# Attention with a relative bias, then a mixture of adapters: a new order of the opening's transfers and key tiles, and 1 KB pieces of k for seven more pairs

## The chip, the cores and the metric

The kernel runs on one core of one Trainium2 chip. The metric is the device time of one execution in microseconds (us), as the median of several runs; less is better.

## The reference

```python
# attention: q, k, v are (B=8, H=8, S=576, D=64) fp32, bias_table is (32, 8)
scores = q @ k.T / sqrt(64)                       # per batch and head, 576 x 576
bucket = f(abs(i - j))                            # 32 buckets, the last one from distance 128 on
scores = scores + bias_table[bucket]              # per head
attn = exp(scores - max); attn = attn / sum
attn_out = attn @ v
# mixture of adapters: x is attn_out as (N=4608, Dm=512); 8 experts of rank 16, two per row
logits = x @ w_gate                               # (512, 8)
w = softmax over the two largest logits of a row
delta = sum over the two chosen e of w_e * (x @ A[e]) @ B[e]
out = x + delta                                   # (4608, 512) fp32
```

The bias depends only on the distance between two positions, and from 128 on it is one constant per head, which cancels in the softmax.

## The kernel before

**Units of work.** Two heads of one batch are a pair; there are 32 pairs, `u` = 0 to 31, four per batch. Of the 576 positions of a head, 512 are the main part, worked on as four tiles of 128 keys in the order `KO = (0, 3, 1, 2)`; the other 64 are the tail. The tail's 64 keys against all main queries, and its 64 queries against all main keys, are the "edges" of a pair; tail against tail is a "corner".

**What is done for one pair.** `load` issues the transfers of q, k and v on SP's DMA queue into staging buffers (four per tensor). `cast` makes bf16 of them, on POOL for most pairs. `turn` has TensorE (PE) transpose k and q, with the tails and what the adapters need, into a PSUM score tile (L396), and VectorE (DVE) copies the result to SBUF as `tx` (L401). `keys(u, c)` makes the scores of one key tile (L459), adds the bias by further matmuls from the table `W` (L464), and has ScalarE (ACT) take the exponential (L467, into `pk`). `edges(u)` does the same for the edges (L516, L519, exponential L521 into `pt`), whose bias is multiplied in afterwards by `edge_l` on POOL (L526) and `edge_t` on DVE. `step(u, j)` makes the values of one half of the queries (L545, L553, L562, L564 into `pv`), divides by the sums on DVE (L584, L585, giving the rows `xn`) and takes in pieces of the adapters' work (L592, L648).

**Shared memory.** There are three PSUM score tiles, used in a ring by `keys`, `edges` and `turn`. Two further PSUM banks (`mm`) are shared by the values, the adapters' products and the edge factors. v has three bf16 buffers.

**Two ways to load k.** q, and the k of the pairs below `WHOLE = 10`, are loaded with one transfer of 256 KB in which partition p holds positions 4p to 4p+3, so that each piece is 1 KB. v, and k from pair 10 on, are loaded with two transfers of 128 KB in pieces of 256 B, in which partition p holds positions p, 128+p, 256+p and 384+p. A k that was loaded whole has to be put in order: in `turn`, its item is then named `keys_done`, the copy to SBUF is split in two, and the first part (L399, 512 elements per partition) reorders the four key blocks while the second (L401) copies the rest.

**The bias table.** It is built on chip, written to a DRAM buffer `g_d`, and read back for the second to fourth pair of each batch by `table(h)` (L212, two transfers into `Wt`, issued on SP). From `Wt`, ACT makes exponentials for the edge factors (`near_first` for the first pair; `near_rows`, L206, for the other three), and POOL makes a reordered copy `W` by `split_table` (L216), which the bias matmuls of all pairs but the first read. `factors_l` makes the edge factors `EL` and `EC` with small matmuls into both `mm` banks (L238, L244) and DVE copies (L248); `factors_t` makes `ET` in the same manner (L257).

**Order.** The order on every engine is written out by hand: each engine runs its instructions in the order of the program text, and SP issues its transfers in that order. The opening is a list of calls. Its transfers stand in one block:

```python
load(2, "qk")
load(0, "v"); load_tail(0, "v")
for h in range(2): table(h)
load(3, "qk"); load(1, "v"); load(4, "qk"); ...
```

and behind the turn of the third pair the calls follow in the order that the diff shows. From pair 2 to pair 29 a loop runs: casts of pair u+2, issue of the loads of q and k of pair u+4 and v of pair u+3, key tiles 0, 3 and 1 of pair u, `step(u-1, 0)`, key tile 2, `turn` of pair u+2, the edges of pair u+1, `step(u-1, 1)`. A pair's turn is thus done two passes before its keys are. The edges of pair u+1 stand inside `turn`, behind its copies, save where the flag `behind` is true: there the turn brings the tails of a batch whose first pair is u+1, and the edges follow `step(u-1, 1)`. That is so at u = 3 alone, since the tails of the later batches are turned a pass or more ahead of their first use.

Of the kernel before, what the change touches and what calls it, by code (L numbers as in the profile page):

```python
# [37 lines left out]
def kernel(  # L38
# [11 lines left out]
    nc = tc.nc  # L50
# [38 lines left out]
    NU = len(units)  # L89


    WHOLE = 10
    NV = 3
    PT = 64 + 2 * SM
    vts = [cp.tile([128, 4, 2, W1], BF16, name=f"v{i}", tag=f"v{i}") for i in range(NV)]
# [6 lines left out]
    def load(u, names="qkv", eng=nc.sync):  # L102
        b, hp = units[u]
        for nm in names:
            src = {"q": q, "k": k, "v": v}[nm]
            t = stg.tile([128, 2, 4 * D], FP32, name=f"{nm}s", tag=f"{nm}s")
            heads = src[b, 2 * hp:2 * hp + 2, :SM, :]
            if nm == "v" or (nm == "k" and u >= WHOLE):
                for h in range(2):
                    eng.dma_start(out=t[:, h, :].rearrange("p (c d) -> p c d", c=4),  # L110
                                  in_=heads[h].rearrange("(c p) d -> p c d", c=4))
            else:
                eng.dma_start(out=t, in_=heads.rearrange("h (p c) d -> p h (c d)", c=4))
            stage[(u, nm)] = t
# [17 lines left out]
    def cast(u, nm, eng):  # L132
        s = stage[(u, nm)].rearrange("p h (c d) -> p h c d", c=4)
        if nm == "v":
            t = vts[u % NV]
            eng.tensor_copy(t[:, :, :, :D].rearrange("p c h d -> p h c d"), s)  # L136
        else:
            t = qkp.tile([128, 4, 2, D], BF16, name=f"{nm}n", tag=f"{nm}n")
            copy = eng.copy if eng is nc.scalar else eng.tensor_copy
            copy(t.rearrange("p c h d -> p h c d"), s)  # L140
            nat[(u, nm)] = t
# [69 lines left out]
    def table(h):  # L211
        nc.sync.dma_start(out=Wt[h * 64:h * 64 + 64, 1:],  # L212
                          in_=_dram(gd, (h * HP + 1) * GL, [[1, 64], [GL, HP - 1], [1, WN]]))
# [37 lines left out]
    def factors_t(g0, g1):  # L251
        ps = [mp.tile([128, 512], FP32, name="ft", tag="mm") for _ in range(2)]
        for hp in range(g0, g1):
            o = (hp - g0) * 64
            for f in range(2):
                for h in range(2):
                    nc.tensor.matmul(ps[h][f * 64:f * 64 + 64, o:o + 64], lhsT=turned(h),  # L257
                                     rhs=table_row(slice(h * 64, h * 64 + 64), hp, 256 - 64 * f),
                                     start=(hp == g0), stop=True, skip_group_check=True)
        for h in range(2):  # L260
            nc.vector.tensor_copy(ET[:, g0:g1, h, :],
                                  ps[h][:, :64 * (g1 - g0)].rearrange("p (g x) -> p g x", g=g1 - g0))
# [107 lines left out]
            t.group, t.k = g, k  # L370
        return g

    def turn(items, copy=nc.vector.tensor_copy, corner=None, after=None, first=None, fill=0):
        n = sum(it[1] for it in items)
        n0 = 4 if items[0][0].__name__ == "keys_done" else 0
        assert n <= (16 if corner is None else 12)
        pf = score_tile("tx")
        ps = pf.rearrange("p a x -> p (a x)").bitcast(BF16).rearrange("p (a x) -> p a x", a=2)
        if corner is not None:
            cs = pf[:, :, 384:]  # L380
            corner_scores(corner, lambda hp: cs[:, hp // 2, (hp % 2) * 64:(hp % 2) * 64 + 64],
                          lambda hp: hp % 2 == 0)
        sb = txp.tile([128, 16, 2, 64], BF16, name="tx", tag="tx")
        s0 = 0
        for _, k, src, quarter in items:
            keep_busy(fill if s0 else 0)
            for i in range(k):
                c = s0 + i
                for a in range(2):
                    rows = slice(a * 64, a * 64 + 64)  # L390
                    cols = slice(c * 64, c * 64 + 64)
                    if quarter:
                        for h in range(2):
                            nc.tensor.transpose(ps[h * 64:h * 64 + 64, a, cols], src(i, a, h), ident[rows, rows])
                    else:
                        nc.tensor.transpose(ps[:, a, cols], src(i, a), ident[rows, rows])  # L396
            s0 += k
        if n0:
            (first or copy)(sb[:, :4].rearrange("p c a i -> p (c a i)").rearrange("p (a i c) -> p a i c", a=2, c=4),  # L399
                            ps[:, :, :256].rearrange("p a (c i) -> p a i c", c=4))  # L400
        copy(sb[:, n0:n], ps.rearrange("p a (c i) -> p c a i", i=64)[:, n0:n])  # L401
        if after is not None:
            after()
        if corner is not None:
            pxs[corner] = ep.tile([128, HP, 64], BF16, name="pcx", tag="pcx")
            nc.scalar.activation(pxs[corner].rearrange("p (a g) i -> p a (g i)", a=2), cs, ACT.Exp, scale=scale)  # L406
        s0 = 0
        for done, k, *_ in items:
            done(sb, s0)
            s0 += k  # L410

    def qk_item(u):
        n = [nat.pop((u, nm)) for nm in ("k", "q")]

        def done(sb, s0):
            qkT[u] = sb[:, s0:s0 + 8].rearrange("p (n c) a i -> p n (c a i)", n=2)

        def keys_done(sb, s0):
            done(sb, s0)
        return keys_done if u < WHOLE else done, 8, lambda i, a: n[i // 4][a * 64:a * 64 + 64, i % 4].rearrange("p h d -> p (h d)"), False  # L420

    def tl_item(b, g0=0, g1=HP):
        n = nat[(b, "qk")]
# [263 lines left out]
    nc.sync.dma_start(out=gd, in_=gx)  # L687
    load_tail(0, "qk", 2)
    load(2, "qk")
    load(0, "v")  # L690
    load_tail(0, "v")
    for h in range(2):
        table(h)
    load(3, "qk")
    load(1, "v")
    load(4, "qk")
# [28 lines left out]
    keys(0, KO[2])  # L725
    turn([qk_item(2), tl_item(0, 2, HP)])
    factors_t(0, 1)
    cast(0, "v", nc.gpsimd)
    cast_tail(0, "v", nc.gpsimd)
    keys(0, KO[3])  # L730
# [1 line left out]
    px = corners_first(0)  # L732
    corners_bias(0, px, 0, 1)
    edges(2)
    split_table(1, nc.gpsimd)
    near_rows(0)
    near_rows(1)
    step(0, 0)
    keys(1, KO[0])
    split_table(2, nc.gpsimd)  # L740
    cast(3, "q", nc.gpsimd)
    cast(3, "k", nc.gpsimd)
    keys(1, KO[1])
    step(0, 1)
    keys(1, KO[2])
    factors_l(1, HP)
    cast(1, "v", nc.gpsimd)
    keys(1, KO[3])
# [93 lines left out]
    for u in range(2, NU - 2):  # L842
        b, hp = units[u]
        prep(u)
        if u == 2:
            cast(2, "v", nc.gpsimd)
            split_table(3, nc.gpsimd)
        if u == 4:
            weights_cast()
        if u == 3:  # L850
            split_table(0, nc.gpsimd)
            nc.gpsimd.memset(sel, 0.0)
            nc.gpsimd.affine_select(out=sel, in_=sel, compare_op=ALU.not_equal, fill=1.0, base=-4,
                                    pattern=[[1, 4 + Dm]], channel_multiplier=-4)
        if u + 4 < NU:
            load(u + 4, "qk")
        if u == 2:
            weights_load()
        if u in tload:
            load_tail(tload[u], "qk")  # L860
        if u + 3 < NU:
            load(u + 3, "v")
        if u in tvload:
            load_tail(tvload[u], "v")
        if u == 7:
            weights_out()
        for c in KO[u == 2:3]:
            keys(u, c)
            if c == KO[0] and u - 1 in tcorner:
                ring[:2] = ring[1::-1]  # L870
        if u == 5:
            weights_turn(1)
        zs = za.pop(u, [None])
        edge_l(u)
        edge_t(u)
        step(u - 1, 0, da.pop(u, []), z=zs[0], zt=ta.pop(u, [None])[0])
        prep_late(u)
        if u == 9:
            nc.gpsimd.tensor_copy(Bc, Bf)
        keys(u, KO[3])  # L880
        if u == 4:
            weights_turn(0)
        items = []
        if u + 2 < NU:
            items.append(qk_item(u + 2))
        if u in tturn:
            items.append(tl_item(tturn[u]))
        for fn, bb, i in xt.pop(u, []):
            items.append(fn(tile_for(bb, i)))
        def next_edges():  # L890
            open_probs(u + 1)
            edges(u + 1)

        behind = u in tturn and tturn[u] == units[u + 1][0]
        turn(items, corner=tcorner.get(u), after=None if behind else next_edges)
        zs = zb.pop(u, [None])
        step(u - 1, 1, db.pop(u, []), z=zs[0], zt=tb.pop(u, [None])[0])
        if behind:
            next_edges()
        if u in tv:  # L900
            cast_tail(tv[u], "v", nc.gpsimd)
        for bb, i in wq.pop(u, []):
            moe_w(groups[(bb, i)])
        if u in tcorner:
            corners_bias(tcorner[u], pxs.pop(tcorner[u]))
# [217 lines left out]
```

## Time and profile before

| | before |
|---|---|
| runs | 185.55, 185.67, 186.34 us; median 185.67 |
| profiled execution: its own time, its span | 187.19 us, 185.4 us |
| TensorE (PE) busy | 171.7 us (93% of the span) |
| ScalarE (ACT) busy | 163.3 us (88%) |
| VectorE (DVE) busy | 136.7 us (74%) |
| GpSimd (POOL) busy | 113.0 us (61%) |
| main DMA queue (q1) | 38.16 MB in 87,940 packets, 79.9% of 16 engines' span |
| granted TensorE clock, mean | 0.992 |

The span runs from the first to the last instruction of the profiled execution; its own time also has what lies around the span, and this one execution took longer than the median of the runs. A row of the costliest groups reads: line, engine, operation, result <- operand (partitions x elements, type), count | busy time, mean ns of one | idle time of the engine just before these instructions, and what ended most of it. A row of a timeline reads: start in us, busy time, engine, line, operation, result <- operand, count, and in brackets the idle time before it with what ended it. A row of the DMA issues has the size of one transfer and the median time from issue to landing. The slices cut the span into 40 parts of 4.6 us.

### The profile page before, as it was taken

How to read it: one execution, taken by the hardware profiler on the slowest of the kernel's cores; microseconds unless marked ns; L12 is line 12 of the kernel's file. 1: busy time of each engine (PE TensorE's matmuls, PEld its weight loads, DVE VectorE, ACT ScalarE, POOL GpSimd, SP SyncE). 2: the span in 40 equal slices, each digit the busy share in tenths (PEclk: the TensorE clock that was granted, in tenths of full speed). 3: DMA queues.
4: the chain of work that ended last, by engine and by line, in shares of the span. 5: the costliest groups of instructions: out<-in, count | busy, mean ns of one | idle time of the engine just before them, and what ended most of it. 6: DMA issues, size and time to landing. Idle time of an engine off the chain costs nothing.

```text
span 185.4 us, 9934 instructions
## 1 busy us (share of the span) xinstructions
PE 171.7 (93%) x4276; PEld 122.5 (66%) x4276; DVE 136.7 (74%) x359; ACT 163.3 (88%) x199; POOL 113.0 (61%) x253
## 2 busy tenths in 40 slices
PE   7877797999999999999999999999999999999980
PEld 2435475776666776777777777677667677788950
DVE  6663876687756786779887897779776888788780
ACT  2397988999899999999999999999989989987880
POOL 8336689287379835984398527945398648435230
PEclk9999999999999999999999999999999999999996
DMA  5899989998999997899899688798998976333336
GB/s 140 213 245 264 241 220 235 205 223 237 225 240 219 228 236 203 209 241 229 212 232 256 172 227 237 188 241 215 266 255 225 265 186 179 118 117 114 119 150 246
DMA packets 88627, 39.26 MB, mean 212 GB/s; under 512 B 72576, under 2 KB 83848, under 8 KB 88584
## 3 DMA queue, kind: packets, MB, share of 16 engines
q1 hardware_dynamic: 87940, 38.16, 79.9%
q8 instruction: 33, 0.54, 1.4%
q10 hardware_dynamic: 644, 0.48, 1.2%
q14 instruction: 10, 0.08, 0.1%
HBM read 29.10 MB, written 9.44 MB: 208 GB/s over the span
## 4 chain that ended last, share of the span: by engine, by line
PE 59%; ACT 13%; DMA 8%; POOL 7%; SPq 4%; issue 4%; DVE 3%; POOLq 0%; ACTq 0%; DVEq 0%
PE pv L545 12%; ACT pk L467 11%; PE sc L459 11%; PE tx L396 5%; PE sc L464 4%; PE dl L648 4%; PE sc L516 3%; PE sc L519 3%; DMA qkt<-in_k_dram 3%; PE pv L562 3%; PE pv L553 3%; PE pv L592 3%; DMA vs<-in_v_dram 2%; ACT pt L521 2%; DMA qkt<-in_q_dram 2%
## 5 line engine op out<-in xcount | busy, mean ns | idle before, releaser
L467 ACT ACTIVATE pk<-sc 128x1024 bf16<-128x1024 f32 x120 | 113.3, 1028 | 5.4 <-PE sc L464 4.9
L459 PE MATMUL sc<-tx 64*64 64x512 bf16 x480 | 44.3, 389 | 1.0 <-ACT pt L521 0.6
L545 PEld LDWEIGHTS <-pk 128*128 128x128 bf16 x1024 | 37.6, 97 | 8.9 <-issue 2.3
L545 PE MATMUL pv<-v,pk 128*128 128x65 bf16 x992 | 41.3, 193 | 0.0
L521 ACT ACTIVATE pt<-sc 128x1024 bf16<-128x1024 f32 x32 | 33.5, 1046 | 3.8 <-PE sc L519 2.8
L464 PE MATMUL sc<-W,anti 64*64 64x192 bf16 (+1 forms) x464 | 34.2, 276 | 0.0
L401 DVE COPY tx<-tx 128x2048 bf16<-128x2048 bf16 (+7 forms) x34 | 32.0, 942 | 1.2 <-PE tx L396 1.0
L585 DVE TENSOR_TENSOR xn<-pv,rc 128x320 bf16<-128x320 f32 x62 | 30.5, 491 | 2.1
L584 DVE RECIPROCAL rc<-pv 128x5 f32<-128x5 f32 x62 | 12.0, 193 | 19.9 <-PE pv L592 11.4
L140 POOL CAST kn<-ks 128x512 bf16<-128x512 f32 x30 | 18.6, 621 | 10.2 <-DMA ks<-in_k_dram 10.2
L459 PEld LDWEIGHTS <-tx 64*64 64x64 bf16 x480 | 15.4, 105 | 11.9 <-issue 1.5
L319 DVE TENSOR_TENSOR ot<-dl,xn 128x512 f32<-128x512 f32 x25 | 17.2, 687 | 7.5 <-PE dl L648 7.4
L136 POOL CAST v<-vs 128x512 bf16<-128x512 f32 x32 | 20.6, 644 | 3.1 <-PE pv L564 2.3
L526 POOL TENSOR_TENSOR pt<-pt,EL 128x128 bf16<-128x128 bf16 x32 | 13.7, 429 | 11.3 <-ACT pt L521 7.7
L505 POOL TENSOR_TENSOR pc<-pcx,EC 128x256 bf16<-128x256 bf16 (+2 forms) x9 | 5.6, 617 | 23.3 <-ACT pcx L406 16.1
L140 POOL CAST qn<-qs 128x512 bf16<-128x512 f32 x30 | 18.4, 614 | 1.0 <-DMA qs<-in_q_dram 1.0
L553 PE MATMUL pv<-vb,pt 128*128 128x130 bf16 x124 | 17.4, 223 | 1.2 <-POOL vb L151 1.2
L562 PE MATMUL pv<-v,pt 128*128 128x65 bf16 x248 | 17.8, 194 | 0.0
L464 PEld LDWEIGHTS <-anti 64*64 64x64 bf16 x480 | 15.0, 106 | 0.2 <-issue 0.2
L562 PEld LDWEIGHTS <-pt 128*128 128x128 bf16 x256 | 14.1, 98 | 0.1
L592 PE MATMUL pv<-AW,tx 128*128 128x136 bf16 x124 | 12.5, 224 | 0.0
L396 PEld LDWEIGHTS <-kn 64*128 64x128 bf16 x256 | 5.7, 94 | 10.2 <-issue 4.9
(151 smaller groups left out, 296.6 us busy)
## 6 DMA issues: line engine op xcount, KB each, us to landing
qs<-in_q_dram SPq DMA_DIRECT2D x32, 256.0 KB, 4.3
vs<-in_v_dram SPq DMA_DIRECT2D x64, 128.0 KB, 4.1
out_dram<-ot SPq DMA_DIRECT2D x32, 256.0 KB, 3.4
ks<-in_k_dram SPq DMA_DIRECT2D x44, 128.0 KB, 4.2
ks<-in_k_dram SPq DMA_DIRECT2D x9, 256.0 KB, 5.3
vt<-in_v_dram SPq DMA_DIRECT2D x8, 128.0 KB, 4.6
qkt<-in_q_dram SPq DMA_DIRECT2D x7, 128.0 KB, 4.4
qkt<-in_k_dram SPq DMA_DIRECT2D x7, 128.0 KB, 4.5
```

The lines of the kernel that those rows point to most:

```text
L136: eng.tensor_copy(t[:, :, :, :D].rearrange("p c h d -> p h c d"), s)
L140: copy(t.rearrange("p c h d -> p h c d"), s)
L401: copy(sb[:, n0:n], ps.rearrange("p a (c i) -> p c a i", i=64)[:, n0:n])
L459: nc.tensor.matmul(sc[prt, h, :], lhsT=kT[rows, c * 128 + f * 64:c * 128 + f * 64 + 64], rhs=qT[rows, :], start=True, stop=False, skip_gro ...
L464: nc.tensor.matmul(_ap(sc[prt, h, :], p0, [[128, 4], [1, n]]), lhsT=turned(h), rhs=band(rows, u, y0, 0, 1, n), start=False, stop=True, ski ...
L467: nc.scalar.activation(probs[u][0][:, c, :, :], sc, ACT.Exp, scale=scale)
L521: nc.scalar.activation(probs[u][1][:, 64:], sc.rearrange("p h x -> p (h x)"), ACT.Exp, scale=scale)
L545: nc.tensor.matmul(pv[:, o:o + W1], lhsT=pk_slice(u, c, h, j + 2 * f), rhs=vm[:, c, h, :], start=first, stop=False, skip_group_check=True)
L553: nc.tensor.matmul(_ap(pv, h * W1, [[130, 2], [1, W1]]), lhsT=probs[u][1][:, x0:x0 + 128], rhs=tvs[b % 2][:, 2 * hp + h].rearrange("p f d ...
L562: nc.tensor.matmul(pv[:, o:o + W1], lhsT=probs[u][1][:, x0:x0 + 128], rhs=vts[u % NV][:, c, h, :], start=False, stop=False, skip_group_che ...
L585: nc.vector.tensor_tensor(xs[b][:, j, hp], _ap(pv, 0, [[W1, 5], [1, D]]), _ap(rc, 6 * j, [[1, 5], [0, D]]), op=ALU.mult)
L592: nc.tensor.matmul(pv[:, o:o + ER + E], lhsT=t.xT[c], rhs=AW[:, c, :], start=first and c == cs[0], stop=(c == HP - 1), skip_group_check=True)
```

## The change

Five edits:

1. `WHOLE` becomes a list: the pairs below 10, and 12, 13, 17, 20, 21, 25 and 29. Their k is loaded by one transfer in 1 KB pieces, and their turns, which run at u = 10, 11, 15, 18, 19, 23 and 27, have the reordering copy.
2. `turn` gets a flag `late`: with it the reordering copy follows the plain copy. It is set where `behind` is, at u = 3.
3. The two transfers of `table` are issued ahead of the first v and the tail of v.
4. `split_table(1)` and `split_table(2)` stand on POOL ahead of the cast of the first v.
5. The second pair's first two key tiles stand ahead of the first values (`step(0, 0)`), and its third tile stands between `step(0, 0)` and `step(0, 1)`; before, the first, second and third tile stood behind `step(0, 0)`, behind the casts of the fourth pair, and behind `step(0, 1)`.

```diff
-    WHOLE = 10
+    WHOLE = [u for u in range(B * HP) if u < 10 or u in (12, 13, 17, 20, 21, 25, 29)]
...
-            if nm == "v" or (nm == "k" and u >= WHOLE):
+            if nm == "v" or (nm == "k" and u not in WHOLE):
                 for h in range(2):
                     eng.dma_start(out=t[:, h, :].rearrange("p (c d) -> p c d", c=4),
                                   in_=heads[h].rearrange("(c p) d -> p c d", c=4))
...
-    def turn(items, copy=nc.vector.tensor_copy, corner=None, after=None, first=None, fill=0):
+    def turn(items, copy=nc.vector.tensor_copy, corner=None, after=None, first=None, fill=0, late=False):
...
-        if n0:
+        def in_order():
             (first or copy)(sb[:, :4].rearrange("p c a i -> p (c a i)").rearrange("p (a i c) -> p a i c", a=2, c=4),
                             ps[:, :, :256].rearrange("p a (c i) -> p a i c", c=4))
+        if n0 and not late:
+            in_order()
         copy(sb[:, n0:n], ps.rearrange("p a (c i) -> p c a i", i=64)[:, n0:n])
+        if n0 and late:
+            in_order()
...
-        return keys_done if u < WHOLE else done, 8, lambda i, a: ...
+        return keys_done if u in WHOLE else done, 8, lambda i, a: ...
...
     load_tail(0, "qk", 2)
     load(2, "qk")
+    for h in range(2):
+        table(h)
     load(0, "v")
     load_tail(0, "v")
-    for h in range(2):
-        table(h)
     load(3, "qk")
...
     turn([qk_item(2), tl_item(0, 2, HP)])
     factors_t(0, 1)
+    for i in (1, 2):
+        split_table(i, nc.gpsimd)
     cast(0, "v", nc.gpsimd)
     cast_tail(0, "v", nc.gpsimd)
     keys(0, KO[3])
...
     edges(2)
-    split_table(1, nc.gpsimd)
     near_rows(0)
     near_rows(1)
-    step(0, 0)
     keys(1, KO[0])
-    split_table(2, nc.gpsimd)
+    keys(1, KO[1])
     cast(3, "q", nc.gpsimd)
     cast(3, "k", nc.gpsimd)
-    keys(1, KO[1])
+    step(0, 0)
+    keys(1, KO[2])
     step(0, 1)
-    keys(1, KO[2])
     factors_l(1, HP)
...
-        turn(items, corner=tcorner.get(u), after=None if behind else next_edges)
+        turn(items, corner=tcorner.get(u), after=None if behind else next_edges, late=behind)
```

More of the change, by code (lines that the diff above doesn't have):

```diff
@@ L419, in keys_done @@
             done(sb, s0)
-        return keys_done if u < WHOLE else done, 8, lambda i, a: n[i // 4][a * 64:a * 64 + 64, i % 4].rearrange("p h d -> p (h d)"), False
+        return keys_done if u in WHOLE else done, 8, lambda i, a: n[i // 4][a * 64:a * 64 + 64, i % 4].rearrange("p h d -> p (h d)"), False
     def tl_item(b, g0=0, g1=HP):
```

## The prediction

> **What bounds the kernel now.** I read the page first (busy times, the slices, the costliest groups), then the timelines of the engines from 8 to 31 us, because most of the diff lies there, then the forms of the tx copies, the DMA issues and the waits of the stretch from 110 to 140 us.
>
> ```profile
> PE 171.7 (93%) x4276; PEld 122.5 (66%) x4276; DVE 136.7 (74%) x359; ACT 163.3 (88%) x199; POOL 113.0 (61%) x253
> GB/s 140 213 245 264 241 220 235 205 223 237 225 240 219 228 236 203 209 241 229 212 232 256 172 227 237 188 241 215 266 255 225 265 186 179 118 117 114 119 150 246
> q1 hardware_dynamic: 87940, 38.16, 79.9%
> L467 ACT ACTIVATE pk<-sc 128x1024 bf16<-128x1024 f32 x120 | 113.3, 1028 | 5.4 <-PE sc L464 4.9
> ```
>
> ScalarE and TensorE pass the lead to each other: the exponentials of the score tiles (L467) are 113.3 us, and in 120 of them ACT sat idle for only 5.4 us ahead of them, nearly all of it waiting for PE. Once the pairs run, neither has much to give; what an edit can win is an idle stretch of ACT that nothing else refills. A microsecond is 0.54% of the time here, and 0.5% (0.93 us) is about what a measurement of this kernel can tell from no change. The profiled execution took 187.19 us, of which 185.4 are the span and 1.8 lie around it; the median of the runs is 185.67. My terms are differences within the span, so I add them to the median.
>
> The opening, where the first idle stretch lies, engine by engine:
>
> ```profile
> 8.20 1.03 SPq L110 DMA_DIRECT2D vs<-in_v_dram  x2
> 9.27 0.60 SPq L122 DMA_DIRECT2D vt<-in_v_dram  x1
> 9.91 1.29 SPq L212 DMA_DIRECT2D Wt<-g_d  x2
> 14.69 1.02 ACT L521 ACTIVATE pt<-sc 128x1024 bf16<-128x1024 f32 x1
> 16.58 0.78 ACT L206 ACTIVATE Wn<-Wt 128x384 bf16<-128x384 bf16 x2 [0.86 <-DMA Wt<-g_d]
> 17.50 6.58 ACT L467 ACTIVATE pk<-sc 128x1024 bf16<-128x1024 f32 x7
> 24.42 1.03 ACT L467 ACTIVATE pk<-sc 128x1024 bf16<-128x1024 f32 x1 [0.35 <-PE sc L464]
> 12.95 0.62 POOL L136 CAST v<-vs 128x512 bf16<-128x512 f32 x1 [0.58 <-DMA vs<-in_v_dram]
> 15.53 0.86 POOL L151 CAST vb<-vt 64x512 bf16<-64x512 f32 x1 [1.97 <-DMA vt<-in_v_dram]
> 16.36 0.30 POOL L505 TENSOR_TENSOR pc<-pcx,EC 128x64 bf16<-128x64 bf16 x1
> 16.63 0.88 POOL L216 COPY W<-Wt 128x320 bf16<-128x320 bf16 x2
> 16.45 0.28 PE L553 MATMUL pv<-vb,pt 128*128 128x130 bf16 x2 [1.20 <-POOL vb L151]
> 16.85 0.41 PE L459 MATMUL sc<-tx 64*64 64x512 bf16 x4
> 17.68 0.67 PE L545 MATMUL pv<-v,pk 128*128 128x65 bf16 x16
> 18.66 0.19 DVE L584 RECIPROCAL rc<-pv 128x5 f32<-128x5 f32 x1 [0.99 <-PE pv L564]
> 18.89 0.49 DVE L585 TENSOR_TENSOR xn<-pv,rc 128x320 bf16<-128x320 f32 x1
> 19.43 0.25 PE L238 MATMUL fl<-anti,Wn 64*64 64x32 bf16 x7 [0.32 <-DVE xn L585]
> 19.93 0.36 DVE L248 CAST EL<-fl 128x192 bf16<-128x192 f32 x1 [0.55 <-PE fl L244]
> 22.30 0.41 PE L459 MATMUL sc<-tx 64*64 64x512 bf16 x4 [0.41 <-DVE tx L401]
> ```
>
> Two transfers end waits here at nearly the same time: the tail of v at 15.5 (POOL's cast of it, then PE's first use at 16.45 after 1.20 us idle) and the bias table at 16.58 (ACT, 0.86 idle).
>
> **The opening: table ahead of v, two key tiles ahead of the values.** The table's two issues leave SP at 8.20 instead of 9.91, and the two issues of the first v and that of its tail come 1.29 us, with the gap 1.33, later. The queue was serving 245 to 264 GB/s in the slices from 9.3 to 18.5 us, so 256 KB of v and 128 KB of tail are 1.5 us of it: the table then lands at about 16.58 - 1.5 = 15.1, before ACT has finished the edge tile (14.69 + 1.02 = 15.71). The wait of 0.86 goes; ACT does the near rows (0.78) until 16.5 and starts the second pair's tiles there, 1.0 us earlier than 17.50.
>
> What is late next is the tail of v. The table is 240 KB, 0.95 us of the same queue, now ahead of it: 15.5 becomes 16.45. POOL is free by then: the two table splits (0.88), which it now does before the first v's cast, end at 15.1 + 0.88 = 16.0, and the cast of v, landed at 12.95 + 0.95 = 13.9, at 16.6, so at most 0.15 more; I count PE's L553 at 16.45 + 0.95 = 17.40. Behind it stand, in PE's order, the rest of the first values (16.85 - 16.45 = 0.40), then one key tile where there were two (16.85 to 17.68 for two, so 0.42 for one), and from the second values' start to the edge factors 19.43 - 17.68 = 1.75, because the factors need both PSUM banks and so wait for DVE's L584 and L585. Sum 2.57 after 17.40, which is 19.97 against 19.43: the factors come **0.54 later**. ACT has three tiles to work on meanwhile (16.5 to about 19.3) and then waits for the fourth, which PE makes right behind the factors: 17.50 + 3 x 0.94 = 20.3 becomes 20.8. From the factors on the shift isn't absorbed: DVE works from EL (19.93) through the copies of the next turn, for which PE waits at 22.30, and at 24.42 ACT waits 0.35 for PE. So two tiles are earlier, but the stretch ends later. Bounds: if the tail isn't delayed at all, 2.57 - 2.98 = -0.41; if it comes by the whole displacement of its issue, 1.33 - 0.41 = +0.92. I take +0.54, which rests on the queue's own rate. The later loads keep their place: what is moved past each other is v, its tail and the table alone, in total the same bytes.
>
> **The turn of the third pair (late=behind).** Only one turn is both a batch's tail turn and ahead of that batch's first pair, u = 3.
>
> ```profile
> 26.48 3.77 ACT L467 ACTIVATE pk<-sc 128x1024 bf16<-128x1024 f32 x4
> 29.04 0.69 DVE L399 COPY tx<-tx 128x512 bf16<-128x512 bf16 x1 [0.37 <-PE tx L396]
> 29.65 0.68 DVE L401 COPY tx<-tx 128x1024 bf16<-128x1024 bf16 x1
> 29.68 0.19 PE L564 MATMUL pv<-vb,pc 128*128 128x65 bf16 x1
> 30.38 0.29 PE L516 MATMUL sc<-tx 64*128 64x64 bf16 x8 [0.51 <-DVE tx L401]
> 31.01 1.02 ACT L521 ACTIVATE pt<-sc 128x1024 bf16<-128x1024 f32 x1 [0.75 <-POOL qn L140]
> ```
>
> The edge tile of pair 4 needs the tails, which are in the second copy (L401). PE idled 0.51 for it; the profile puts ACT's 0.75 down to a POOL cast, but L521 follows PE's edge matmuls by 0.63 and needs them. With L401 first it ends at 29.04 + 0.68 = 29.72; PE is busy with the values until 29.68 + 0.19 = 29.87, so the edges start at 29.90 and the exponential at 30.53, after ACT is free (26.48 + 3.77 = 30.25): **0.48 earlier**. Both copies end when they did, so the PSUM tile is free as before, and the keys in L399 are not used before the next turn. Bounds: 0 (edges wait for the whole tile) to -0.75 (all of ACT's wait).
>
> **1 KB pieces of k for pairs 12, 13, 17, 20, 21, 25, 29.** One issue of 256 KB replaces two of 128 KB, and each of their turns gets the reordering copy L399 beside a shorter L401.
>
> ```profile
> ks<-in_k_dram SPq DMA_DIRECT2D x44, 128.0 KB, 4.2
> ks<-in_k_dram SPq DMA_DIRECT2D x9, 256.0 KB, 5.3
> L399 DVE COPY tx<-tx 128x512 bf16<-128x512 bf16 x10 | 6.9, 689 | 3.4 <-PE tx L396 3.2
> L401 DVE COPY tx<-tx 128x1536 bf16<-128x1536 bf16 x7 | 6.6, 948 | 0.0
> L401 DVE COPY tx<-tx 128x1024 bf16<-128x1024 bf16 x5 | 3.4, 680 | 0.0
> 105.50 0.19 DVE L584 RECIPROCAL rc<-pv 128x5 f32<-128x5 f32 x1 [0.39 <-PE pv L564]
> 110.79 0.19 DVE L584 RECIPROCAL rc<-pv 128x5 f32<-128x5 f32 x1
> 114.03 0.62 POOL L140 CAST kn<-ks 128x512 bf16<-128x512 f32 x1 [1.20 <-DMA ks<-in_k_dram]
> 116.37 0.23 ACT L621 ACTIVATE th<-sm 128x32 f32<-128x32 f32 x1 [0.38 <-POOL sm L612]
> 134.58 0.62 POOL L140 CAST kn<-ks 128x512 bf16<-128x512 f32 x1 [1.43 <-DMA ks<-in_k_dram]
> 137.02 0.24 ACT L621 ACTIVATE th<-sm 128x40 f32<-128x40 f32 x1 [0.67 <-POOL sm L612]
> ```
>
> DVE's price: 689 + 680 - 948 = 0.42 us for a turn that had a 1536-element copy, 0.34 where the second copy starts 0.08 before the first ends, as at 29.04 and 29.65. What hides it is DVE's wait for PE ahead of the next reciprocal: 0.39 at 105.50, but none at 110.79, behind the turn that feeds pair 21. Without cover it costs up to 0.34 a turn. The gain: k arrives sooner only where somebody waits for it. POOL's casts wait for k at 114.03 (pair 23) and 134.58 (pair 27), and through POOL's order the gate's tanh on ACT comes 0.38 and 0.67 late. Neither pair is among the seven, and their loads are issued after stores that wait for computed rows, so an emptier queue is all that they get. Together I take **0.0**: bounds -1.05 (both waits gone) and +2.4 (seven copies of 0.34 uncovered).
>
> Sum: +0.54 - 0.48 + 0.0 = +0.06, 185.67 + 0.06 = **185.7 us**: two edits of the opening that undo each other.
>
> **The rivals.** *The queue becomes short enough (faster).* Seven loads in a quarter of the packets relieve a queue whose packets fill 79.9% of 16 engines' span; the loads behind them land earlier, also those of pairs 23 and 27, and the tanh waits of 0.38 and 0.67 go: 185.7 - 1.05 = 184.6. For it: both waits end with a landing of k, and the queue is nearly full. Against: 256 KB at once took 5.3 us to land, not less than 4.2 for a half, though those nine loads are of the crowded opening. It decides if POOL's sm is no later than the end of ACT's edge tile. The Trainium skill (DMA: Bandwidth & Descriptors, Why small descriptors are slow) speaks for this rival: it counts 3 cycles of overhead on 8 of data for a 256-byte descriptor, so 11 cycles against 8.75 for the same bytes in 1 KB; by that, an estimate from its figures, each load takes a fifth less transfer time. No row here shows the price of one packet by its size.
>
> *The second copy is on the path (slower).* If DVE's cover is thinner than the one row that I show, the reciprocals slip by 0.34, the PSUM bank of the values comes free later, and PE, at 93%, waits: 7 x 0.34 = 2.4, 188.1; with half of the turns 186.9. It decides where the wait ahead of L584 is below 0.34. Against: 0.39 at 105.50; for: 110.79.
>
> *The late copy doesn't free the edges (it doesn't do what it says).* If the wait covers the whole tile, 0.48 is missing: 186.2.
>
> **How the numbers follow.** The forecast has 0.53, its own range from the opening's bounds 184.9 to 186.1. The faster rival 0.27, the slower one 0.12, the missing late gain 0.08. Faster by over 0.5% (below 184.74) holds the faster rival and the forecast's lowest edge: 0.28. Slower (above 186.60) holds the slower rival and 0.05 of the others, where the opening's upper bound adds to a missing gain or to an uncovered copy: 0.17. Within 0.5%: 0.55. The range for 8 in 10 reaches down past the faster rival, which may come with an opening better than 0.54, to 184.3, and up to the slower one's half price, 186.9.
>
> **What would show it.** Right, if in the new profile ACT has no wait for Wt at the near rows and starts the second pair's tiles near 16.5; the tail of v is cast near 16.45, PE's L553 starts near 17.4 and the fl matmuls near 20.0; ACT is idle over 1 us ahead of the second pair's fourth tile; the edge matmuls of pair 4 follow the values without a wait for L401; and tanh still waits for POOL near 116 and 137. Wrong, if the tail of v lands as early as before (opening -0.4), if the waits for k on POOL and of tanh are gone (faster), or if DVE's waits ahead of L584 behind the seven turns shrink to nothing and ACT's waits for L464 grow there (slower).

## The result, and the profile after

| | before | changed |
|---|---|---|
| runs, median | 22 runs: 186.72 us (184.95 to 191.10) | 22 runs: 188.47 us (185.91 to 190.74) |
| ratio to before, 95% interval | | **1.0073** (1.0044 to 1.0103) |
| profiled execution: its own time, its span | 187.19 us, 185.4 us | 187.24 us, 185.5 us |

The kernel became slower by 0.73%, some 1.4 us (0.8 to 1.9). The forecast was no change, 185.7 us, with 186.9 as the upper end; the ratio on the forecast's base, 185.67 us, is 187.0, so it was wrong. The ratios here and below compare undisturbed runs alone, so they are not quotients of the medians. The two profiled executions differ by 0.05 us only: that of before took longer than the median of its runs, that of the changed kernel less. So the result can't be read from this pair alone.

The page of the changed kernel, the lines that answer to those shown of before:

```profile
PE 172.0 (93%) x4276; PEld 122.6 (66%) x4276; DVE 141.3 (76%) x366; ACT 163.4 (88%) x199; POOL 112.4 (61%) x253
q1 hardware_dynamic: 82452, 38.16, 77.6%
L471 ACT ACTIVATE pk<-sc 128x1024 bf16<-128x1024 f32 x120 | 113.5, 1030 | 7.5 <-PE sc L468 6.9
ks<-in_k_dram SPq DMA_DIRECT2D x16, 256.0 KB, 4.8
ks<-in_k_dram SPq DMA_DIRECT2D x30, 128.0 KB, 5.3
```

Below `turn` the lines are numbered four higher (L467 is L471, L531 is L535); within it, L401 is L403. The queue carries the same bytes in fewer packets, 77.6% for 79.9%; DVE works 4.6 us more; and ACT's idle time ahead of the exponentials rose from 5.4 to 7.5 us. The timelines of the changed kernel show where that is (start, busy time, engine, and in brackets the idle time before it with what ended it):

```profile
15.74 0.76 ACT L206 ACTIVATE Wn<-Wt 128x384 bf16<-128x384 bf16 x2
16.40 1.93 ACT L471 ACTIVATE pk<-sc 128x1024 bf16<-128x1024 f32 x2
19.09 1.02 ACT L471 ACTIVATE pk<-sc 128x1024 bf16<-128x1024 f32 x1 [0.76 <-PE sc L468]
21.59 3.77 ACT L471 ACTIVATE pk<-sc 128x1024 bf16<-128x1024 f32 x4 [1.47 <-PE sc L468]
26.62 1.02 ACT L525 ACTIVATE pt<-sc 128x1024 bf16<-128x1024 f32 x1
15.98 0.81 POOL L151 CAST vb<-vt 64x512 bf16<-64x512 f32 x1
16.75 0.30 POOL L509 TENSOR_TENSOR pc<-pcx,EC 128x64 bf16<-128x64 bf16 x1
17.00 0.60 POOL L140 CAST qn<-qs 128x512 bf16<-128x512 f32 x1
17.56 0.60 POOL L140 CAST kn<-ks 128x512 bf16<-128x512 f32 x1
15.76 0.55 DVE L151 CAST vb<-vt 64x512 bf16<-64x512 f32 x1 [1.69 <-DMA vt<-in_v_dram]
16.34 1.90 DVE L535 TENSOR_TENSOR pt<-pt,ET 128x128 bf16<-128x128 bf16 x1
16.84 0.28 PE L557 MATMUL pv<-vb,pt 128*128 128x130 bf16 x2
18.30 0.23 PE L566 MATMUL pv<-v,pt 128*128 128x65 bf16 x2 [1.12 <-DVE pt L535]
18.49 0.41 PE L463 MATMUL sc<-tx 64*64 64x512 bf16 x4
18.97 0.67 PE L549 MATMUL pv<-v,pk 128*128 128x65 bf16 x16
20.72 0.24 PE L238 MATMUL fl<-anti,Wn 64*64 64x32 bf16 x7 [0.68 <-DVE xn L589]
```

ACT no longer waits for the table, and the second pair's tiles start at 16.40. But DVE's `edge_t` of the first pair (L535), a multiplication that reads two SBUF operands, took **1.90 us**, where it took 0.51 before:

```profile
15.96 0.51 DVE L531 TENSOR_TENSOR pt<-pt,ET 128x128 bf16<-128x128 bf16 x1
17.46 0.61 POOL L140 CAST qn<-qs 128x512 bf16<-128x512 f32 x1
18.02 0.61 POOL L140 CAST kn<-ks 128x512 bf16<-128x512 f32 x1
```

In the changed kernel it started at 16.34 while POOL was at work and ended at 18.24, just after POOL's row of four instructions had ended (17.56 + 0.60 = 18.16). Before, POOL's row had no gap either: tail cast, corner, two splits and these two casts follow one another from 15.53 to 18.63. Yet `edge_t` was done at 16.47, 0.08 us after the first of them, the tail cast (15.53 + 0.86 = 16.39). In the changed kernel PE's next matmuls (L566) need its result and came 1.12 us late; ACT then waited 0.76 and 1.47 us for PE. The same instruction over the whole span, before and changed, from the view of one line (min/median/max in ns):

```profile
L531 DVE TENSOR_TENSOR pt<-pt,ET x32: 205/292/689, 16.0 to 167.9; 128x128 bf16<-128x128 bf16 x32
```

```profile
L535 DVE TENSOR_TENSOR pt<-pt,ET x32: 204/344/1895, 16.3 to 167.8; 128x128 bf16<-128x128 bf16 x32
```

One and the same operation on the same shape took from 0.2 to 1.9 us: its work is the same, so the rest is time in which it is counted as started and doesn't get on.

### The profile page after: what moved, and what is told of

It is laid out like the page before. It is cut to its first block, busy times and chain, and to the rows that moved or that the text cites. A ratio compares the mean times of both kernels' runs of the same rounds, so it can differ in the third digit from the quotient of the medians.

```text
span 185.5 us, 9929 instructions
## 1 busy us (share of the span) xinstructions
PE 172.0 (93%) x4276; PEld 122.6 (66%) x4276; DVE 141.3 (76%) x366; ACT 163.4 (88%) x199; POOL 112.4 (61%) x253
## 3 DMA queue, kind: packets, MB, share of 16 engines
q1 hardware_dynamic: 82452, 38.16, 77.6%
## 4 chain that ended last, share of the span: by engine, by line
PE 69%; ACT 14%; DVE 6%; DMA 4%; SPq 3%; issue 2%; ACTq 0%; DVEq 0%
PE pv L549 15%; PE sc L463 13%; ACT pk L471 12%; PE tx L396 6%; PE sc L468 5%; PE dl L652 4%; PE sc L520 4%; PE pv L566 4%; PE sc L523 3%; PE pv L557 3%; PE pv L596 3%; DMA vt<-in_v_dram 3%; ACT pt L525 2%; DMA btT<-in_bias_table_dram 1%; DVE pt L535 1%
## 5 line engine op out<-in xcount | busy, mean ns | idle before, releaser
L471 ACT ACTIVATE pk<-sc 128x1024 bf16<-128x1024 f32 x120 | 113.5, 1030 | 7.5 <-PE sc L468 6.9
L403 DVE COPY tx<-tx 128x2048 bf16<-128x2048 bf16 (+7 forms) x34 | 30.2, 888 | 1.0 <-PE tx L394 0.4
L566 PE MATMUL pv<-v,pt 128*128 128x65 bf16 x248 | 18.0, 194 | 1.1 <-DVE pt L535 1.1
L557 PE MATMUL pv<-vb,pt 128*128 128x130 bf16 x124 | 17.4, 223 | 0.1
L566 PEld LDWEIGHTS <-pt 128*128 128x128 bf16 x256 | 14.1, 98 | 1.4 <-DVE pt L535 1.2
L535 DVE TENSOR_TENSOR pt<-pt,ET 128x128 bf16<-128x128 bf16 x32 | 13.5, 425 | 0.9 <-ACT pt L525 0.5
L399 DVE COPY tx<-tx 128x512 bf16<-128x512 bf16 x17 | 11.6, 684 | 3.3 <-PE tx L396 3.2
```

What stands on the lines that cost most here:

```text
L471: nc.scalar.activation(probs[u][0][:, c, :, :], sc, ACT.Exp, scale=scale)
L557: nc.tensor.matmul(_ap(pv, h * W1, [[130, 2], [1, W1]]), lhsT=probs[u][1][:, x0:x0 + 128], rhs=tvs[b % 2][:, 2 * hp + h].rearrange("p f d ...
L566: nc.tensor.matmul(pv[:, o:o + W1], lhsT=probs[u][1][:, x0:x0 + 128], rhs=vts[u % NV][:, c, h, :], start=False, stop=False, skip_group_che ...
```

## The experiments

Each was timed against the kernel before in five rounds, in three sets (e1 to e4, e5 to e8, e9 to e12); the second set ran on another chip than the other two.

**One part at a time.** e1 is the kernel before with edits 3, 4 and 5; e2 has edit 2 alone, e3 edit 1 alone. e4 is the changed kernel with one line moved:

```diff
     cast(0, "v", nc.gpsimd)
+    edge_t(0)
     cast_tail(0, "v", nc.gpsimd)
     keys(0, KO[3])
-    edge_t(0)
```

> The kernel before with edits 3, 4 and 5 alone (table and splits ahead of v, two key tiles ahead of the first values). Theory A (a held-up DVE): in the new profile the first pair's edge multiplication on DVE (edge_t) took 1.90 us beside POOL's casts and PE waited 1.12 us for it; if that happens in most executions, this kernel has the whole loss of the opening, 1.3 us, and is 1.0 to 1.4 us slower than before. Theory B (whole k): the hold-up was a chance of one execution, the opening costs 0.0 to 0.5, and the loss sits in the loop, in the second copies of the seven turns.

> The kernel before with edit 2 alone (the reordering copy last, in the turn at u = 3). Both theories: 0.5 us faster (0.58 in the new profile, from 1.28 late at the edges of pair 3 to 0.70 at those of pair 4). If it gives nothing, the gain is handed back later in the loop.

> The kernel before with edit 1 alone (1 KB pieces of k for pairs 12, 13, 17, 20, 21, 25, 29). Theory A: the new profile regains 0.74 us between the edges of pairs 15 and 26, so this kernel is 0.3 to 0.8 us faster. Theory B: 0.6 to 1.6 us slower, 0.1 to 0.2 for each of the seven copies.

> The changed kernel with the first pair's edge_t ahead of the cast of the tail of v on DVE, so that it runs near 14.1 us, when POOL is idle, and needs no late landing. Theory A: the wait of 1.12 us of PE ahead of L566 goes, and the kernel is 0.9 to 1.2 us faster than the changed one, so within 0.4 us of the kernel before. Theory B: it goes too, but in most executions it was not there, and the time stays 1 us or more above the kernel before.

| | ratio to before | 95% interval |
|---|---|---|
| e1 opening alone | 1.0090 | 1.0054 to 1.0127 |
| e2 late copy alone | 0.9980 | 0.9951 to 1.0009 |
| e3 whole k alone | 0.9977 | 0.9944 to 1.0010 |
| e4 changed, edge_t first | 0.9978 | 0.9935 to 1.0021 |

The opening alone is 1.7 us slower (1.0 to 2.4); the others are not clear of no change, both on the faster side. In e1 L535 again took 1.89 us and PE again waited 1.12. In e4 it ran while POOL was idle, and PE did not wait for it:

```profile
13.73 0.23 DVE L535 TENSOR_TENSOR pt<-pt,ET 128x128 bf16<-128x128 bf16 x1
16.31 0.28 PE L557 MATMUL pv<-vb,pt 128*128 128x130 bf16 x2 [0.49 <-POOL vb L151]
16.42 0.28 PE L566 MATMUL pv<-v,pt 128*128 128x65 bf16 x4
```

Theory A stands, and theory B falls: one line, which changes neither the transfers nor the order on PE, takes the ratio from 1.0073 to 0.9978. The two come from different sets of runs; their distance of 0.95% is 1.8 us, more than the 1.12 of the one wait, but 1.12 lies within what the two intervals leave.

**Is it POOL, or the late landing?** e4 takes away both a late start and POOL's company. e5 leaves `edge_t` in its place and moves POOL's casts of pair 3 behind its cast of the second v. e7 keeps the changed order of transfers and splits, and goes back to the old order of key tiles. e6 has edits 1 and 2 without the opening; e8 is the kernel before with `edge_t` first. The cut shows e5:

```diff
     keys(1, KO[1])
-    cast(3, "q", nc.gpsimd)
-    cast(3, "k", nc.gpsimd)
     step(0, 0)
...
     cast(1, "v", nc.gpsimd)
+    cast(3, "q", nc.gpsimd)
+    cast(3, "k", nc.gpsimd)
     keys(1, KO[3])
```

> The changed kernel with POOL's casts of q and k of pair 3 behind its cast of the second v, nothing else. POOL then has nothing to do between its corner multiplication and the landing of the second v (17.1 to 18.3 in the profile of the changed kernel). If it is POOL's uninterrupted run of casts that holds up DVE's edge_t, edge_t ends near 17.1 instead of 18.24, PE's wait of 1.12 falls below 0.2, and the kernel is 0.9 to 1.2 us faster than the changed one. Rival (edge_t is late because the tail of v lands late): edge_t and PE's wait stay as they are, no change.

> Edits 1 and 2 alone, the opening as before. By the single runs (late 0.2% faster, whole k 0.23% faster): 0.8 us faster than before, range 0.4 to 1.1, and 0.4 us faster than the changed kernel with edge_t first if the opening, without the hold-up, still costs my 0.54; 0.5 us slower than that one if the opening without the hold-up gains, as the single profile has it (edges of pair 3 at 24.85 against 25.34 before).

> The changed kernel with the old order of the second pair's key tiles (the first values ahead of both), the table's transfers and splits as changed. If the hold-up comes from POOL having its splits behind it, so that its tail cast, corner and casts run without a wait: edge_t takes 1.5 to 2 us here too, and the kernel is as slow as the changed one or up to 0.8 us slower, since PE now waits ahead of the two key tiles. Rival (the key tiles ahead of the values make the loss): at the time of the kernel before or faster.

> Control: the kernel before with edge_t of the first pair ahead of the cast of the tail of v. In its profile edge_t took 0.51 us and nobody waited for it: no change, within 0.3 us. If it is over 0.5 us faster, the hold-up also happens in the kernel before, in executions that its one profile does not show.

| | ratio to before | 95% interval |
|---|---|---|
| e5 changed, casts later | 0.9981 | 0.9946 to 1.0017 |
| e6 edits 1 and 2 | **0.9926** | 0.9887 to 0.9965 |
| e7 table ahead, old key order | 1.0096 | 1.0054 to 1.0138 |
| e8 before, edge_t first | 0.9973 | 0.9935 to 1.0011 |

e5's timelines:

```profile
15.95 0.42 DVE L151 CAST vb<-vt 64x512 bf16<-64x512 f32 x1 [1.99 <-DMA vt<-in_v_dram]
15.98 0.86 POOL L151 CAST vb<-vt 64x512 bf16<-64x512 f32 x1 [0.21 <-DMA vt<-in_v_dram]
16.41 0.51 DVE L535 TENSOR_TENSOR pt<-pt,ET 128x128 bf16<-128x128 bf16 x1
16.81 0.29 POOL L509 TENSOR_TENSOR pc<-pcx,EC 128x64 bf16<-128x64 bf16 x1
18.40 0.62 POOL L136 CAST v<-vs 128x512 bf16<-128x512 f32 x1 [1.29 <-DMA vs<-in_v_dram]
17.01 0.28 PE L566 MATMUL pv<-v,pt 128*128 128x65 bf16 x4
```

The tail of v landed as late as in the changed kernel and `edge_t` started as late (16.41), but with the two casts moved away it took 0.51 us instead of 1.90, and PE's wait is gone. It ended at 16.92, 0.08 us after the tail cast (15.98 + 0.86 = 16.84), while POOL was still in the corner. So the late landing alone doesn't hold it up; with POOL's two casts behind the corner it is held up. e7 shows the other half:

```profile
15.78 1.89 DVE L535 TENSOR_TENSOR pt<-pt,ET 128x128 bf16<-128x128 bf16 x1
16.43 0.60 POOL L140 CAST qn<-qs 128x512 bf16<-128x512 f32 x1
16.98 0.61 POOL L140 CAST kn<-ks 128x512 bf16<-128x512 f32 x1
17.73 0.29 PE L566 MATMUL pv<-v,pt 128*128 128x65 bf16 x2 [0.97 <-DVE pt L535]
18.90 1.94 ACT L471 ACTIVATE pk<-sc 128x1024 bf16<-128x1024 f32 x2 [2.79 <-PE sc L468]
```

The old order of key tiles doesn't help: with the splits ahead, POOL has its tail cast, corner and two casts in one row, and L535 takes 1.89 us again. So edit 5 isn't needed for the hold-up. The clock granted to PE was 0.53 from 14 to 20 us in this profile (1.00 in the changed kernel), so ACT's wait of 2.79 is not the hold-up's alone. The first profile of the kernel before has the same order of key tiles and a tail that came nearly as late (its cast starts at 15.50, here at 15.32), but the splits between corner and casts, and there L531 took 0.51. That points to edit 4, which takes the splits out from between; no run has edit 3 without edit 4, so their shares are not shown. In e8 nobody waited for `edge_t` and the time is not clear of before, as expected of the control. e6 beats both kernels: 1.4 us faster than before (0.7 to 2.1), more than the 0.8 that the sum of e2 and e3 gave, though its interval holds that.

**What the opening is worth without the hold-up, and whether whole k does anything.** e9 is e6 with `edge_t` first; e10 the kernel before again; e11 is e4 again, now in the same set as e9; e12 has edit 1 alone, for all pairs below 30. The cut shows e12 against the changed kernel, whose edits 2 to 5 it leaves out too:

```diff
-    WHOLE = [u for u in range(B * HP) if u < 10 or u in (12, 13, 17, 20, 21, 25, 29)]
+    WHOLE = list(range(30))
```

> Edits 1 and 2 with the first pair's edge_t ahead of the cast of the tail of v, the opening otherwise as before. From the two parts (edits 1 and 2: 0.74% faster; edge_t first on the kernel before: 0.27%, not clear of nothing): 1.0 us faster than before, range 0.5 to 1.9. It should be the fastest of all kernels here.

> The kernel before once more, as a control and for a second profile. Time: no change, within 0.5%. If the late landing of the tail of v (cast on DVE at 15.50 after a wait of 1.55) belongs to the one profiled execution, the tail's cast starts near 14.3 here without a wait for a transfer, as in four kernels that have the old order of transfers (14.19 to 14.45), and the first fl matmuls of the second to fourth pair start at 18.0 to 18.9 instead of 19.43. If it is the rule, the new profile shows 15.3 to 15.6 again.

> The changed kernel with edge_t first, once more, beside the kernel that differs from it by the opening's edits 3, 4 and 5 alone. If the opening costs something even without the hold-up, since the tail of v now waits behind the table in every execution, it is 0.4 to 1.2 us slower than that one. If the hold-up was the whole loss, the two agree within 0.3 us.

> Edit 1 for all pairs below 30, 20 pairs beyond the first ten instead of 7, without the other edits. Theory C (the freed queue gains a little, as the 0.23% of the seven suggests): 0.8 to 1.3 us faster than before. Theory D (the seven's 0.23% is noise, the copies cost where DVE has no time): no change to 2 us slower, with DVE's wait ahead of its reciprocals shrinking by 0.3 us a turn.

| | ratio to before | 95% interval |
|---|---|---|
| e9 edits 1 and 2, edge_t first | 0.9948 | 0.9913 to 0.9983 |
| e10 before again | 0.9997 | 0.9955 to 1.0038 |
| e11 as e4 | 0.9982 | 0.9940 to 1.0023 |
| e12 whole k for 20 more pairs | 0.9990 | 0.9952 to 1.0028 |

e9 is faster than before, but not, as expected, the fastest of all (e6 has 0.9926): with the old opening, `edge_t` first adds nothing that can be seen. e11 is 0.34% slower than e9, some 0.6 us, in the direction and within the size that an opening which costs something by itself would have, but the intervals overlap. e10's opening is the more telling part, the kernel before in a second execution:

```profile
14.27 0.42 DVE L151 CAST vb<-vt 64x512 bf16<-64x512 f32 x1
14.73 0.79 DVE L531 TENSOR_TENSOR pt<-pt,ET 128x128 bf16<-128x128 bf16 x1
15.13 0.30 POOL L505 TENSOR_TENSOR pc<-pcx,EC 128x64 bf16<-128x64 bf16 x1
15.38 0.88 POOL L216 COPY W<-Wt 128x320 bf16<-128x320 bf16 x2
15.90 0.77 ACT L206 ACTIVATE Wn<-Wt 128x384 bf16<-128x384 bf16 x2
16.57 7.54 ACT L467 ACTIVATE pk<-sc 128x1024 bf16<-128x1024 f32 x8
18.27 0.24 PE L238 MATMUL fl<-anti,Wn 64*64 64x32 bf16 x7 [0.32 <-DVE xn L585]
```

Neither of the two waits that the prediction started from is here: the tail of v is cast at 14.27 without a wait, the table is there in time, and the eight exponentials from 16.57 on run without a gap. Of the eight kernels with the old order of transfers (before, e2, e3, e6, e8, e9, e10, e12) only the first profile has a wait of DVE for the tail of v; its cast starts at 13.98 to 14.60 in the other seven and at 15.50 there.

e12's groups of DVE, and below them those of before (copies; its L399 has 6.9 us) and of e10 (reciprocals):

```profile
L403 DVE COPY tx<-tx 128x1536 bf16<-128x1536 bf16 (+6 forms) x34 | 26.6, 783 | 0.0
L399 DVE COPY tx<-tx 128x512 bf16<-128x512 bf16 x30 | 20.7, 689 | 4.0 <-PE tx L396 3.4 <-PE tx L394 0.2
L588 DVE RECIPROCAL rc<-pv 128x5 f32<-128x5 f32 x62 | 11.9, 192 | 16.0 <-PE pv L596 10.1 <-PE pv L568 5.1
```

```profile
L401 DVE COPY tx<-tx 128x2048 bf16<-128x2048 bf16 (+7 forms) x34 | 32.0, 942 | 1.2 <-PE tx L396 1.0
L584 DVE RECIPROCAL rc<-pv 128x5 f32<-128x5 f32 x62 | 12.0, 193 | 19.5 <-PE pv L592 11.4 <-PE pv L564 7.4
```

The copies rose by 26.6 + 20.7 - 38.9 = 8.4 us, 0.42 for each of the 20 turns; DVE's wait ahead of its reciprocals gave 3.5 of them (19.5 to 16.0). The queue's share fell from 81.3% (e10) to 76.9%. The time did not move. Theory C falls; of theory D it is the end "no change" that holds.

## Why the prediction was wrong, step by step

**The table and the start of the second pair: right.** No wait at the near rows (forecast: it goes), tiles from 16.40 (forecast 16.5).

**The tail of v: right in direction, on a poor base.** The forecast had PE's L553 (now L557) at 17.40, and it was at 16.84: the tail landed nearly as late in the old profile as in the new. Against the other seven profiles of the old order the displacement is larger: DVE's cast of the tail starts at 15.26 to 15.98 in the six profiles with the new order (the changed kernel, e1, e4, e5, e7, e11), against 13.98 to 14.60, on average 1.3 us later, for the 0.95 that I took and the 1.33 of my upper bound.

**From there to the edge factors: the step that failed.** I added "the rest of the first values (16.85 - 16.45 = 0.40)", then 0.42 for one key tile, then 1.75 to the factors. Measured: 18.49 - 16.84 = **1.65**, then 0.48, then 1.75. The 0.40 holds only if `edge_t` is done by then, and no term of the sum has `edge_t` in it. Its 0.51 us of the old trace is partly a wait already (it takes 0.23 beside an idle POOL). I costed edit 4 by when the splits and casts of POOL end, and not by whom they keep out. Where `edge_t` is not held up, the step holds: from L557 to the factors it is 2.64 us in each of e4, e5 and e11 (forecast 2.57), and 3.88 in the changed kernel and in e1, so the hold-up costs 1.24 of this path. So the factors came at 20.72, where 19.97 was forecast, and ACT's fourth tile at 21.59, where 20.8 was.

**The size of the opening without that: open.** The edge tile of pair 3 on ACT is the first instruction behind the opening. In the eight profiles with the old order of transfers it starts at 25.34, 25.51, 25.74, 24.79, 23.75, 24.13, 24.00 and 23.68, mean 24.62; with the changed opening and the hold-up at 26.62 and 26.71 (the changed kernel, e1); with the changed opening and no hold-up at 24.85, 25.43 and 24.75 (e4, e5, e11), mean 25.01. By these means the changed opening without the hold-up costs 25.01 - 24.62 = 0.39, and the hold-up the other 1.65. But the three latest of the eight have something of their own: the first the late tail of v, e2 and e3 a granted clock of 0.72 from 14 to 20 us, where the other five and the three without hold-up have 1.00. The five have a mean of 24.07, and against them the opening costs 0.94. The forecast +0.54 lies between the two; that is no proof of it. The ratios too say that it costs something (e4, e5, e11 at 0.9978 to 0.9982; e6 and e9 at 0.9926 and 0.9948).

**The late copy: right.** From the edge tile of pair 3 to that of pair 4 the old profile has 31.01 - 25.34 = 5.67 us, the changed one 5.09: 0.58 earlier, forecast 0.48. It is the most regular effect here: 5.09 or 5.10 in seven of the eight profiles with edit 2 (e7 has 5.36), 5.66 or 5.67 in the six without it. The rows of the changed kernel:

```profile
30.31 0.69 DVE L403 COPY tx<-tx 128x1024 bf16<-128x1024 bf16 x1 [0.37 <-PE tx L396]
30.92 0.68 DVE L399 COPY tx<-tx 128x512 bf16<-128x512 bf16 x1
31.09 0.29 PE L520 MATMUL sc<-tx 64*128 64x64 bf16 x8
31.71 1.02 ACT L525 ACTIVATE pt<-sc 128x1024 bf16<-128x1024 f32 x1 [0.18 <-issue]
```

PE starts the edges 0.13 us after the start of the last of the values (L568, 30.96), and no longer waits for the copies. The time of e2 alone, 0.20% faster, is 0.37 us (0.9 faster to 0.2 slower), which holds 0.58.

**Whole k: right at zero, and both rivals fall.** The price of 0.42 us a turn was right; nearly three times as many such turns changed nothing, so DVE had the room. The tanh waits that the faster rival was to win (0.38 and 0.67) are gone in the changed kernel, where I had forecast them to stay, but also in e1 and e2, which have k as before; e10 has two others (0.41 and 0.26), and e11, with the seven pairs, one of 1.23 at 137.88. They come and go with the execution. The lighter queue that the rival needed is real, but no gain in time came of it.

**The sum.** Forecast +0.54 - 0.48 + 0.0; measured by parts +1.67 - 0.37 - 0.43 = +0.9, and together +1.4 (0.8 to 1.9). With e6 (-1.4) in place of e2 and e3 the parts give +0.3; the intervals are too wide to say whether the parts add up. (One sum in the chances is off: the forecast's own lower end is 185.67 - 0.41 - 0.48 = 184.8, not 184.9; nothing hangs on it.) None of my rivals had a DVE instruction held up by POOL; the slower one put its mechanism in the loop, where nothing happened.

The Trainium skill (SBUF — State Buffer, section "SBUF: two separate sides") states that DVE and GpSimd share one pair of SBUF ports under an exclusive lock, that a DVE operation with two SBUF inputs competes for it with a GpSimd operation that reads SBUF, and that the one that starts later is blocked until the other's instruction is done. The traces agree that `edge_t` is blocked: 0.23 us with POOL idle (e4), and 0.51 beside POOL's tail cast, ending 0.08 after it (before, e5). They go beyond the rule in that DVE stayed blocked across the boundaries between four POOL instructions in three profiles (the changed kernel, e1, e7: 1.89 to 1.90). In e10 it took 0.79 and ended 0.08 us behind the second, the corner, with the splits following. That the ports are the cause is argued from the page; shown is that moving POOL's casts or `edge_t` away ends it. By what rule DVE gets in at the first boundary in one case and at none in another is open. A row of POOL instructions without a gap is not enough: before and e10 had one. Nor is a corner with casts right behind it: at 72.34 us of the changed kernel `edge_t` of a later pair met that and was done after 0.72 us, at the first boundary.

## What to carry to other kernels

When a reorder changes what stands in one engine's queue, ask which short instruction of another engine runs beside it: here, with the table's transfers and two table copies moved forward, a 0.2 us multiplication on VectorE had to sit out a whole row of GpSimd instructions, and TensorE paid over 1 us for it. Put a short VectorE operation that TensorE needs at the place where its inputs are ready, and not behind a landing beside a GpSimd burst. And take the stalls of an opening from several executions before spending an edit on them: of eight profiles with the old order of transfers, only the first has the two waits that this change set out from, DVE's for the tail of v and ACT's for the table.

## What was not expected of the hardware

A VectorE tensor_tensor of 128x128 bf16 elements took between 0.20 and 1.90 us, depending on what GpSimd ran beside it, and its row shows it as busy for all of it: the wait isn't in the idle column. Of the 448 executions of this line in the 14 profiles the three of 1.89 to 1.90 stand alone; the next longest took 0.79. The landing of the bias table, issued at 9.8 to 10.7 us in every kernel with the old order, ended between 14.6 and 16.5 us from one execution to another, and the start of the edge tile behind the opening scattered by 2.1 us (23.68 to 25.74); the two latest are those in which the granted clock was 0.72 there.
